# A planned order with a quiet time for attention products during each slot scatter, other planner constants, and second blocks of 288 rows

## The chip, the cores and the metric

One core of one Trainium2 chip runs the whole program in one launch. The metric is the device time of that launch in microseconds (us); the median of the runs counts. The engines are called PE (matrix products), PEld (the loading of PE's stationary operand), DVE (vector), ACT (scalar), POOL (GpSimd) and SP (the engine that issues most DMAs).

## The reference

Three computations follow each other. Shapes: attention on 4 batches, 8 heads, 768 positions of 48 numbers; 3072 tokens of 384 numbers after it; all float32.

```python
for t in range(S):                                   # delta-rule attention, k_n = k / norm
    y[:, :, t] = einsum('bhd,bhde->bhe', q[:, :, t], state)
    v_old = einsum('bhde,bhd->bhe', state, k_n[:, :, t])
    state = state + beta_t * einsum('bhd,bhe->bhde', k_n[:, :, t], v[:, :, t] - v_old)

h = x @ w_in                                         # first MoE: 384 -> 2048 -> 384
x = where(h > 0, h, exp(min(h, 0)) - 1) @ w_out

noisy = x @ w_gate + log1p(exp(x @ w_noise)) * noise # second MoE: 8 experts, top 2
top2, top2_w = two largest of noisy, softmax of the two
for e in range(8):                                   # 384 -> 1024 -> 384 for the rows sent to e
    out[rows of e] += top2_w * (maximum(x[rows of e] @ w1[e], 0) @ w2[e])
```

## The kernel before, in words

The tokens are cut into six groups of 512 (g = 0 to 5), 128 positions of the sequence each. A group passes through these stages.

**Attention.** `front(g)` prepares a group: gram products of the keys (`grams`, matmul at L467), a triangular solve on DVE (`solve`, L514 and L517, 30 steps, and the transposes at L522 and L524), and two merges of the halves of the solution on PE (L548 and L564). `chain(g, c)` then goes through two chunks c of 64 positions: products with the state (S, L634; U, L652), the update of the state (L668) and the outputs (Y, L693), with DVE and ACT work in between (L639, L641, L657, L675). These are many very small matmuls: a gram is 128 of them, a U or a state update 64.

**First MoE.** For each of 16 slices f of the hidden width a step makes nine matmuls (`l1`, L712) into one bank, an activation on ACT and DVE (`elu`, L717 to L735), and the products with w_out (`l2`, L760, L764 and L765, three for each 128 rows). Groups 0 and 1 are worked in halves of 256 rows for f below 8. w_out is split once into two parts, stored to `wod` in DRAM (L390) and read back as `wo` tiles (L383) by `feed`, all of it on the SP queue.

**Routing.** `routing(g)` transposes the rows (L802), makes the gate scores, picks the two best experts on DVE, makes a running count (L876) and, from it, the slot of each row by two matmuls (L880, L881). GpSimd then writes the slots with eight indirect DMAs (L912). The order of the groups is 1, 0, 2, 3, 4, 5.

**Second MoE.** Each expert has room for 832 rows, in blocks of 512 and 320 (`BLK`); a loop for more rows (`overflow`) stands behind and does not run with these inputs, whose counts per expert are 743 to 797. For a block SP fetches the slots as `ids` (L990, L991, L993), GpSimd gathers the rows of x2d into `xg` by up to four indirect DMAs (L998), PE transposes them (L1012), ACT and DVE split them (L1015, L1017), and eight steps of L1 (L712), relu (L745, L750) and L2 follow; in a last chunk of fewer than 128 rows the high and low parts stand side by side in one stationary operand (L760, L762). `combine` scales the rows and adds them to the output through GpSimd (L1041). The first block needs the slots of groups 0 to 4 only, the second blocks those of all six.

**What sets the order.** Nothing is scheduled on the chip. While the program is built, the class `Sched` keeps a clock for PE, ACT and DVE from assumed costs, and takes at each point, among the jobs that could go on, the one that could start first (within `NEAR`) and has the lowest rank. Products have a kind: 0 dense, 1 attention, 2 transposes and routing. The order in which PE, ACT, DVE, POOL and SP get their instructions is the order in which the planner sent the jobs on, and each engine executes its own list in that order. The constants at the head (`FRONT`, `CONV`, `ROUTE`, `EVAC`, `EW`, `RP`, `TURN`, `DMA_RATE`, `EARLY`) are ranks and assumed costs: a new value means another order, not other work.

Of the kernel before, what the change touches and what calls it, by code (L numbers as in the profile page):

```python
# [12 lines left out]
AF = mybir.ActivationFunctionType  # L13
# [4 lines left out]
B, H, S, D = 4, 8, 768, 48  # L18
DM, F1, E, F2 = 384, 2048, 8, 1024
NT = B * S  # L20
NG = 6
# [4 lines left out]
HALF = NP // 2  # L26
NOUT = NT + NPAD
ES = 3200
BLK = (512, 320)
CAP = sum(BLK)  # L30
FRONT = (1, 1.02, 2.68, 3, 3, 3)
ATT = (1, 1, 1, 1, 1, 1)
CONV = (2, 2.5)
NEAR = 0.1
ROUTE = 2.44
EVAC = 1.39
EW = 5.99
AHEAD = 4
DMA_RATE = 0.226
LAG = 2  # L40
EARLY = {6: 8, 8: 9, 10: 10, 12: 11, 21: 12, 23: 13, 25: 14, 27: 15}
RP = 0.61
TURN = 0.25
FETCH = 3.7

F64_TINY = 2.0 ** -15 * 1.125
# [1 line left out]
def PE(cost, *after, n=0, kind=1, m=5, rank=99):  # L48
    return "PE", cost, after, n, kind, rank, (2, 4, 2)[kind] * m
# [7 lines left out]
def wait(*after):  # L57
    return None, 0.0, after, 0, 0, 99, 0
# [30 lines left out]
class Sched:  # L89
# [7 lines left out]
    def __init__(self):  # L97
        self.clock = {"PE": 0.0, "ACT": 0.0, "DVE": 0.0}
        self.words, self.lines = 0, {0: 0.0, 1: 0.0}
        self.jobs, self.count, self.kind, self.banks, self.got, self.now, self.wire = [], 0, 0, [0.0, 0.0], None, 0.0, 0.0  # L100

    def add(self, job, rank):
        self.count += 1
# [10 lines left out]
    def start(self, step):  # L114
        engine, cost, after, n, kind, _, words = step
        t = self.clock[engine] if engine else 0.0
        for a in after:
            if a is not None and not isinstance(a, float):
                a = a.t
            if a is None:  # L120
                return None
            t = max(t, a)
        if n:
            free = sorted(b for b in self.banks if b is not None)
            if len(free) < n:
                return None
            t = max(t, free[n - 1])
        if words:
            t = max(t, self.lines[(self.words + words) // 256] - 0.5)
        return t  # L130
# [59 lines left out]
class Kernel:  # L190
# [81 lines left out]
    def init_out(self):  # L272

        S, m = self.S, 3 * NOUT // 128
        out = self.out.rearrange("(p m) d -> p (m d)", m=NOUT // 128).rearrange("p (m d) -> p m d", d=128)
        yield wait(self.attended[2])
        for i in range(0, m, 15):
            yield wait(S.now + 12.0)
            S.dma(0.98)
            self.nc.sync.dma_start(out[:, i:i + 15], self.zero[:, None, :].to_broadcast([128, 15, 128]))  # L280


    def moe1_alloc(self):
# [75 lines left out]
    def feed(self):  # L359

        nc, S = self.nc, self.S
        x, v = [t.rearrange("p a b -> p (a b)") for t in self.xtile(1, I32)], self.V.rearrange("p c a b -> p (c a b)")
        places = [t[:, 2 * DM * i:2 * DM * i + 2 * DM].bitcast(I32) for t in (*x, v) for i in range(2)]
        places = [places[(f % 4) if f < 12 else 4 + f % 2] for f in range(NP)]
        stored, dead, order = [Event() for _ in range(NP)], [Event() for _ in range(NP)], []
        for n, (*_, f) in enumerate(self.steps):
            order.append((f, n))
            if n in EARLY:
                order.append((EARLY[n], None))
        done = set()  # L370
        for f, n in order:
            if f in done:
                yield wait(self.rw.need(), stored[f])
            else:
                yield wait(self.rw.need(), *([dead[f - 4]] if 4 <= f < 12 else [self.attended[1], *([dead[f - 2]] if f > 13 else [])]
                                             if f >= 12 else []))
            wo, ready, used = self.work.tile([128, 2, DM], FR, name="wo", bufs=4), Event(), self.rw.take()
            if n is not None:
                self.wos[n] = wo, ready, used
                self.fed[n].t = S.now  # L380
            flat = wo.rearrange("p a d -> p (a d)").bitcast(FT)
            if f in done:
                nc.sync.dma_start(flat, self.wod[f])  # L383
                ready.t = S.dma(0.4)
                continue
            done.add(f)
            nc.sync.dma_start(places[f], self.w_out[128 * f:128 * f + 128].bitcast(I32))

            def end(t, f=f, n=n, ready=ready, used=used, flat=flat):
                nc.sync.dma_start(self.wod[f], flat)  # L390
                ready.t, stored[f].t = t, S.dma(0.4)
                if n is None:
                    used.t = stored[f].t
                if f == 11:
                    self.xfree.t = t
                if f == NP - 1:
                    self.load_v(2)
            S.add(self.convert(places[f], wo[:, 0], wo[:, 1], DM, S.dma(0.4), dead[f], end), CONV[f >= 8])

# [354 lines left out]
    def l2(self, gh, gl, wh, wl, acc, n, first, last):  # L754

        nc = self.nc
        nw = wh.shape[-1]
        for t, a in enumerate(acc):
            o = slice(128 * t, 128 * t + 128)
            nc.tensor.matmul(a[:, :nw], gh[:, o], wh, start=first, stop=False)  # L760
            if o.stop > n:
                nc.tensor.matmul(a[:, :nw], gh[:, o], wl, start=False, stop=last)  # L762
            else:
                nc.tensor.matmul(a[:, :nw], gh[:, o], wl, start=False, stop=False)  # L764
                nc.tensor.matmul(a[:, :nw], gl[:, o], wh, start=False, stop=last)  # L765

# [10 lines left out]
    def x2_out(self, g, acc, held, e):  # L777
        nc = self.nc
        for t, (a, free) in enumerate(zip(acc, held)):
            f = yield DVE(0.56, e, self.rx.need()) if g == 0 else ACT(0.49, e, self.rx.need())  # L780
            x2, used = self.x2s()
# [6 lines left out]
            self.x2[g].append((x2, used, f))  # L788
            r0 = NPAD + 512 * g + 128 * t
            nc.sync.dma_start(self.x2d[r0:r0 + 128, :], x2)  # L790
        self.S.add(self.routing(g), 0.5 if g == NG - 1 else ROUTE)

    def gates(self, g):
        nc, S = self.nc, self.S
# [35 lines left out]
    def routing(self, g):  # L830
# [43 lines left out]
        for b in range(1, B):  # L874
            V.tensor_add(ex[:, b], ex[:, b - 1], m[:, b - 1])
        V.tensor_add(self.cum, ex[:, B - 1], m[:, B - 1])  # L876
        e = yield PE(0.1, e, n=1, kind=2)
        k = self.S.got[0]
        pp = self.bank(k)[:, :B * E]
# [54 lines left out]
        if g == NG - 2:  # L934
            self.adj = self.consts.tile([128, E], FT, name="adj")
            V.tensor_scalar(self.adj, pc, -1.0, float(BLK[0]), op0=OP.mult, op1=OP.add)
            V.tensor_scalar(self.adj, self.adj, 0.0, None, op0=OP.max)
        self.routed[g].t = e + 20.0
        self.listed[g].t = e


# [62 lines left out]
    def gathered_t(self, n, xg, xh, xl, at=None):  # L1004
        nc, S = self.nc, self.S
        for t, x in enumerate(xg):
            e = yield PE(0.35, *([at + 1.0 * t] if at else []), n=1, kind=2)
            k = S.got[0]
            m = min(128, n - 128 * t)
            pt = self.bank(k)[:, :DM].rearrange("p (k m) -> p k m", k=3)  # L1010
# [10 lines left out]
    def gather(self, e, i, xs, out):  # L1021
        yield wait(self.routed[NG - 1 if i else NG - 2])
        out.ids, xg = self.fetch(e, i)
        out.t = yield from self.gathered_t(BLK[i], xg, *xs, self.S.now + 8.0)

    def combine(self, n, ids, acc, held=None, e=0.0):
        nc = self.nc
        puts = []
        for t, a in enumerate(acc):
# [1 line left out]
            f = yield DVE(0.6, e)  # L1031
            y = self.m2.tile([128, DM], FT, name="y", bufs=4)
            if m < 128:
                nc.scalar.activation(y[:m], a[m:, :DM], AF.Copy)
                nc.vector.tensor_add(y[:m], y[:m], a[:m, :DM])
                a = y
            nc.vector.tensor_scalar(y[:m], a[:m, :DM], ids.bitcast(FT)[:m, t, 1:2], None, op0=OP.mult)  # L1037
# [225 lines left out]
```

## Time and profile before

| what | value |
|---|---|
| runs | 1235.65, 1234.97, 1241.44 us; median 1235.65 us |
| the profiled execution | 1239.07 us, its span 1237.3 us |
| mean granted TensorE clock | 0.950 of full speed |
| busy in the span | PE 1076.2, PEld 963.6, DVE 717.5, ACT 491.4, POOL 210.4 us |

The span runs from the first to the last instruction of the profiled execution; 1.8 us of its own time lie outside. All terms are taken from that execution. Busy time of PE is given by modelled ends, so a stretch with PE busy in all of its 25 us has no gap that the profile sees.

### The profile page before, as it was taken

How to read it: one execution, taken by the hardware profiler on the slowest of the kernel's cores; microseconds unless marked ns; L12 is line 12 of the kernel's file. 1: busy time of each engine (PE TensorE's matmuls, PEld its weight loads, DVE VectorE, ACT ScalarE, POOL GpSimd, SP SyncE). 2: the span in 40 equal slices, each digit the busy share in tenths (PEclk: the TensorE clock that was granted, in tenths of full speed). 3: DMA queues.
4: the chain of work that ended last, by engine and by line, in shares of the span. 5: the costliest groups of instructions: out<-in, count | busy, mean ns of one | idle time of the engine just before them, and what ended most of it. 6: DMA issues, size and time to landing. Idle time of an engine off the chain costs nothing.

```text
span 1237.3 us, 28286 instructions
## 1 busy us (share of the span) xinstructions
PE 1076.2 (87%) x11780; PEld 963.6 (78%) x11780; DVE 717.5 (58%) x1832; ACT 491.4 (40%) x979; POOL 210.4 (17%) x282
## 2 busy tenths in 40 slices
PE   1173859679997999979989998999999999999995
PEld 1163759568885888868878887889898989899995
DVE  9979898796354894867453644534535353434321
ACT  2343744735633338425625544123424232323210
POOL 3000000000002020020020041424242323232412
PEclk9997789689998999989998998999999999999998
DMA  9123444642367354225223453135654452524313
GB/s 270 32 79 91 168 162 122 226 172 78 101 184 192 87 146 123 66 63 157 65 66 127 147 138 113 14 90 90 169 113 98 89 139 47 145 42 100 48 16 39
DMA packets 93241, 136.55 MB, mean 110 GB/s; under 512 B 35056, under 2 KB 63472, under 8 KB 92528
## 3 DMA queue, kind: packets, MB, share of 16 engines
q1 hardware_dynamic: 80560, 114.14, 31.8%
q0 software_dynamic: 12544, 20.51, 9.8%
q8 instruction: 95, 1.56, 0.5%
q14 instruction: 42, 0.34, 0.1%
HBM read 108.02 MB, written 26.60 MB: 109 GB/s over the span
## 4 chain that ended last, share of the span: by engine, by line
PE 76%; DVE 13%; ACT 3%; issue 3%; DMA 2%; another core or an unknown queue 1%; POOL 0%; SPq 0%; POOLq 0%; DVEq 0%; ACTq 0%
PE ht L712 31%; PE acc L760 12%; PE acc L765 10%; PE acc L764 10%; PE att L693 3%; DVE TR L514 2%; DVE L L517 2%; PE att L634 2%; PE att L652 2%; PE att L467 2%; PE att L1012 1%; DMA xg<-x2d,ids 1%; PE acc L762 1%; DMA V<-in_w_out_dram 1%
## 5 line engine op out<-in xcount | busy, mean ns | idle before, releaser
L712 PE MATMUL ht<-xh,w 128*128 128x512 f32 (+2 forms) x1056 | 326.7, 369 | 6.1 <-ACT w L314 4.0
L712 PEld LDWEIGHTS ht<-xh,w 128*128 128x128 f32 x1056 | 195.0, 192 | 37.8 <-issue 5.2
L750 DVE SCALAR_TENSOR_TENSOR gl<-ht,gh 128x512 fp32r<-128x512 f32 (+1 forms) x128 | 71.4, 558 | 246.9 <-ACT gh L745 239.5
L712 PE MATMUL ht<-xl,w 128*128 128x512 f32 (+2 forms) x528 | 191.6, 363 | 2.2 <-issue 2.2
L745 ACT ACTIVATE gh<-ht 128x512 fp32r<-128x512 f32 (+1 forms) x128 | 66.4, 519 | 281.6 <-PE ht L712 243.9
L760 PE MATMUL acc<-wo,gh 128*128 128x384 f32 x384 | 140.6, 366 | 10.6 <-DMA wo<-wod 9.7
L765 PE MATMUL acc<-wo,gl 128*128 128x384 f32 x384 | 133.6, 348 | 0.0
L764 PE MATMUL acc<-wo,gh 128*128 128x384 f32 x384 | 133.0, 346 | 0.0
L727 DVE SCALAR_TENSOR_TENSOR e<-e,ht 128x512 f32<-128x512 f32 (+1 forms) x112 | 67.8, 608 | 109.0 <-ACT e L725 106.0
L1041 POOL DMA_INDIRECT out_dram<-y,ids x56 | 88.8, 1586 | 218.5 <-DVE y L1037 208.3
L723 ACT ACTIVATE e<-ht 128x512 f32<-128x512 f32 (+1 forms) x112 | 59.8, 536 | 150.7 <-PE ht L712 140.2
L712 PE MATMUL ht<-xh,ew 128*128 128x320 f32 (+1 forms) x384 | 115.7, 359 | 1.0 <-ACT xh L1015 1.0
L712 PEld LDWEIGHTS ht<-xl,w 128*128 128x128 f32 x528 | 101.5, 192 | 12.5 <-issue 2.3
L912 POOL DMA_INDIRECT slots<-pr,si x48 | 47.8, 996 | 358.3 <-DVE si L907 282.2
L733 ACT ACTIVATE gh<-e 128x512 fp32r<-128x512 f32 (+1 forms) x112 | 63.4, 570 | 79.5 <-DVE e L727 78.1
L760 PEld LDWEIGHTS acc<-wo,gh 128*128 128x128 f32 x384 | 75.2, 196 | 17.3 <-issue 7.4
L735 DVE TENSOR_TENSOR gl<-e,gh 128x512 fp32r<-128x512 f32 (+1 forms) x112 | 68.3, 613 | 30.7 <-ACT gh L733 25.8
L760 PE MATMUL acc<-w,gh 128*128 128x384 f32 x224 | 76.8, 343 | 0.9 <-issue 0.9
L712 PEld LDWEIGHTS ht<-xh,ew 128*128 128x128 f32 x384 | 70.2, 190 | 9.0 <-ACT xh L1015 1.5
L760 PE MATMUL acc<-ew,gh 128*128 128x384 f32 x224 | 77.1, 344 | 0.0
L764 PEld LDWEIGHTS acc<-wo,gh 128*128 128x128 f32 x384 | 75.6, 197 | 1.3
L765 PEld LDWEIGHTS acc<-wo,gl 128*128 128x128 f32 x384 | 75.3, 196 | 0.0
(190 smaller groups left out, 2045.7 us busy)
## 6 DMA issues: line engine op xcount, KB each, us to landing
wo<-wod SPq DMA_DIRECT2D x104, 384.0 KB
ws<-in_w_dram SPq DMA_DIRECT2D x48, 256.0 KB
ws<-in_w_dram SPq DMA_DIRECT2D x64, 192.0 KB
wod<-wo SPq DMA_DIRECT2D x16, 384.0 KB
out_dram<-zero SPq DMA_DIRECT2D x5, 960.0 KB
Kt<-in_kt_dram SPq DMA_DIRECT2D x12, 384.0 KB
w<-in_w_in_dram SPq DMA_DIRECT2D x9, 512.0 KB
SQ<-in_qt_dram SPq DMA_DIRECT2D x24, 192.0 KB
```

The costliest lines, as they stand in the source:

```text
L712: nc.tensor.matmul(ph[:, :n], w(kk, f), x[:, kk, o:o + n], start=(i == 0), stop=(i == 8))
L723: nc.scalar.activation(x, ph[:, :n], AF.Exp)
L727: nc.vector.scalar_tensor_tensor(x, x, -1.0, ph[:, :n], op0=OP.mult, op1=OP.max)
L733: nc.scalar.activation(gh, x, AF.Copy)
L735: nc.vector.tensor_sub(gl, x, gh.bitcast(FT))
L745: nc.scalar.activation(gh[:, :n], ph[:, :n], AF.Relu)
L750: nc.vector.scalar_tensor_tensor(d, ph[:, o], 0.0, gh[:, o].bitcast(FT), op0=OP.max, op1=OP.subtract)
L760: nc.tensor.matmul(a[:, :nw], gh[:, o], wh, start=first, stop=False)
L764: nc.tensor.matmul(a[:, :nw], gh[:, o], wl, start=False, stop=False)
L765: nc.tensor.matmul(a[:, :nw], gl[:, o], wh, start=False, stop=last)
L912: x = nc.gpsimd.indirect_dma_start(out=self.slots[:, :], out_offset=bass.IndirectOffsetOnAxis(ap=si[:, t, b:b + 1], axis=0), in_=pr[:, b, ...
L1041: x = nc.gpsimd.indirect_dma_start(out=self.out[:, :], out_offset=bass.IndirectOffsetOnAxis(ap=ids[:m, t, 0:1], axis=0), in_=y[:m], in_off ...
```

## The change

There are four parts.

1. **A quiet time.** When a routing has updated its running count, the planner notes its time plus `QUIET` = 14 us, and plans no product of kind 1 (attention) before that.
2. **The routing of group 4** gets the rank 0.5 that only group 5 had; the time at which its slots count as readable is `e + 13.0` instead of `e + 20.0`, the transposes of gathered rows are planned from 7 us after the fetch, 1.3 us apart, instead of 8 us and 1.0 us.
3. **Second blocks of 288 rows** instead of 320, with the last chunk's stationary operand cut to the 64 columns that hold data (2 x 32).
4. **Other constants** of the planner, the store of w_out's split parts as a job of its own (`store`, planned 0.21 us before the parts are ready, and so behind DMAs that were sent before it), and the zeros of the output written in 15 pieces, 9 us apart, instead of 5 pieces, 12 us apart.

```diff
-BLK = (512, 320)
+BLK = (512, 288)
-FRONT = (1, 1.02, 2.68, 3, 3, 3)
+FRONT = (1, 1.02, 2.68, 3, 0.62, 3)
-CONV = (2, 2.5)
+CONV = (1.82, 2.5)
-ROUTE = 2.44
-EVAC = 1.39
-EW = 5.99
+ROUTE = 3.7
+EVAC = -0.4
+EW = 4.15
-DMA_RATE = 0.226
+STORE = -0.21
+QUIET = 14.0
+DMA_RATE = 0.244
-EARLY = {6: 8, 8: 9, 10: 10, 12: 11, 21: 12, 23: 13, 25: 14, 27: 15}
-RP = 0.61
-TURN = 0.25
+EARLY = {6: 8, 8: 9, 10: 10, 12: 11, 21: 12, 23: 13, 26: 14, 29: 15}
+RP = 0.91
+TURN = 0.6
...
+        if kind == 1:
+            t = max(t, self.quiet)
...
-        for i in range(0, m, 15):
-            yield wait(S.now + 12.0)
-            S.dma(0.98)
-            self.nc.sync.dma_start(out[:, i:i + 15], self.zero[:, None, :].to_broadcast([128, 15, 128]))
+        for i in range(0, m, 5):
+            yield wait(S.now + 9.0)
+            S.dma(0.33)
+            self.nc.sync.dma_start(out[:, i:i + 5], self.zero[:, None, :].to_broadcast([128, 5, 128]))
...
-            def end(t, f=f, n=n, ready=ready, used=used, flat=flat):
+            def store(t, f, n, used, flat):
+                yield wait(t + STORE)
                 nc.sync.dma_start(self.wod[f], flat)
-                ready.t, stored[f].t = t, S.dma(0.4)
+                stored[f].t = S.dma(0.4)
                 if n is None:
                     used.t = stored[f].t
+
+            def end(t, f=f, n=n, ready=ready, used=used, flat=flat):
+                ready.t = t
+                S.add(store(t, f, n, used, flat), 1)
...
-            nc.tensor.matmul(a[:, :nw], gh[:, o], wh, start=first, stop=False)
             if o.stop > n:
-                nc.tensor.matmul(a[:, :nw], gh[:, o], wl, start=False, stop=last)
+                m = 2 * (n - o.start)
+                o = slice(o.start, o.start + m)
+                nc.tensor.matmul(a[:m, :nw], gh[:, o], wh, start=first, stop=False)
+                nc.tensor.matmul(a[:m, :nw], gh[:, o], wl, start=False, stop=last)
             else:
+                nc.tensor.matmul(a[:, :nw], gh[:, o], wh, start=first, stop=False)
...
-        self.S.add(self.routing(g), 0.5 if g == NG - 1 else ROUTE)
+        self.S.add(self.routing(g), 0.5 if g >= NG - 2 else ROUTE)
...
         V.tensor_add(self.cum, ex[:, B - 1], m[:, B - 1])
+        self.S.quiet = self.S.now + QUIET
...
-        self.routed[g].t = e + 20.0
+        self.routed[g].t = e + 13.0
...
-            e = yield PE(0.35, *([at + 1.0 * t] if at else []), n=1, kind=2)
+            e = yield PE(0.35, *([at + 1.3 * t] if at else []), n=1, kind=2)
...
-        out.t = yield from self.gathered_t(BLK[i], xg, *xs, self.S.now + 8.0)
+        out.t = yield from self.gathered_t(BLK[i], xg, *xs, self.S.now + 7.0)
...
-                nc.scalar.activation(y[:m], a[m:, :DM], AF.Copy)
+                nc.scalar.activation(y[:m], a[m:2 * m, :DM], AF.Copy)
```

**PE after the slot products of group 1's routing.** `att` tiles are the two banks of attention and routing; `ht` is a bank of L1, `acc` of L2. Before (L467 are grams, L668 the update of the state):

```order
L881 MATMUL att_4849<-rex,ones 128x32
L712 MATMUL ht<-xh_2165,w_124 128x512
...
L760 MATMUL acc<-wo,gh 128x384
...
L467 MATMUL att_4914<-Kt_105 32x64 x2
...
L668 MATMUL att_4994<-Ub,Ktm 48x48 x2
```

After the change (L894 is the old L881, L721 the old L712, L775 the old L760, L814 the old L802, L677 the old L668):

```order
L894 MATMUL att_4713<-rex,ones 128x32
L721 MATMUL ht<-xh_2149,w_123 128x512
...
L775 MATMUL acc<-wo,gh 128x384
...
L814 MATMUL att_4781<-ident,x2s 128x128 x3
L721 MATMUL ht<-xh_2149,w_124 128x512
...
L814 MATMUL att_4800<-ident,x2s 128x128 x3
...
L814 MATMUL att_4826<-ident,x2s 128x128 x3
...
L677 MATMUL att_4842<-Ub,Ktm 48x48 x2
```

Before, one L1 and one L2 stood between the slot products and the grams. Now three L1, two L2 and three transposes stand ahead of the first attention product, a state update, and the grams come later still. After the slot products of group 2, too, dense steps now stand where the S products stood, and the first attention product behind them is a merge, as it is after those of group 0. The attention products that stood behind the slot products of group 3 (U, L652, and Y, L693) now stand ahead of them; only dense steps follow there.

**SP around the first two fetches of slots**, at the passage from the first to the second MoE; `ws` are raw pieces of expert weights. Before:

```order
L383 DMA wo<-wod 128x768 x10
L993 DMA ids<-slots 128x4x2
L965 DMA ws<-in_w_dram 128x512 x3
L965 DMA ws<-in_w_dram 128x384 x4
L965 DMA ws<-in_w_dram 128x512 x2
L993 DMA ids<-slots 128x4x2
```

After the change (L387 is the old L383, L978 the old L965, L1006 the old L993):

```order
L387 DMA wo<-wod 128x768 x8
L1006 DMA ids<-slots 128x4x2
L387 DMA wo<-wod 128x768 x3
L978 DMA ws<-in_w_dram 128x512 x3
L978 DMA ws<-in_w_dram 128x384
L1006 DMA ids<-slots 128x4x2
```

The first fetch now stands three `wo` loads, that is three dense steps, ahead of the end of the first MoE; the second behind three `wo` and four `ws` loads instead of nine `ws`. On PE the four transposes of the first block, which before stood in a row ahead of its L1, now stand between half steps of the last group.

**PE at the merges of group 2's front**, still among the half steps of group 1 (L548 and L564 are the merges, L467 the grams of group 3). Before:

```order
L712 MATMUL ht<-xh_2165,w_123 128x256
L548 MATMUL att_2724<-TR,TB_108 32x32 x2
...
L564 MATMUL att_2801<-GD,TR 32x32 x2
...
L467 MATMUL att_2897<-Kt_111 32x64 x2
...
L760 MATMUL acc<-wo,gh 128x384
```

After the change (L557 and L573 are the merges, L476 the grams):

```order
L721 MATMUL ht<-xh_2149,w_123 128x256
L557 MATMUL att_2817<-TR,TB_108 32x32 x2
...
L775 MATMUL acc<-wo,gh 128x384
...
L573 MATMUL att_2946<-GD,TR 32x32 x2
...
L775 MATMUL acc<-wo,gh 128x384
...
L476 MATMUL att_3079<-Kt_111 32x64 x2
```

Before, the first merge, the second and the grams followed each other. Now two half steps, each an L1 and an L2, stand between the merges, and two more between the second merge and the grams.

## Rows read from the trace of the kernel before

**Rows 1.** The page: busy time of each engine, and shares of the chain that ended last.

```profile
PE 1076.2 (87%) x11780; PEld 963.6 (78%) x11780; DVE 717.5 (58%) x1832; ACT 491.4 (40%) x979; POOL 210.4 (17%) x282
...
PE 76%; DVE 13%; ACT 3%; issue 3%; DMA 2%; another core or an unknown queue 1%; POOL 0%; SPq 0%; POOLq 0%; DVEq 0%; ACTq 0%
```

**Rows 2.** Stretches of 25 us: stretch, then busy us of each engine, granted clock, DMA.

```profile
225.00:250.00 25.00, 17.50 (x395) 16.44 (x386) 21.70 (x56) 17.61 (x37) 0.00 (x0) 0.69 0.56 201
...
275.00:300.00 25.00, 25.00 (x245) 22.26 (x239) 21.32 (x46) 9.10 (x16) 0.00 (x0) 0.87 0.22 65
...
450.00:475.00 25.00, 25.00 (x247) 22.16 (x246) 18.18 (x38) 14.67 (x24) 9.22 (x16) 1.00 0.86 198
...
725.00:750.00 25.00, 21.03 (x94) 17.02 (x92) 11.95 (x21) 13.16 (x25) 6.38 (x7) 0.86 0.70 206
750.00:775.00 25.00, 23.52 (x141) 21.12 (x142) 8.72 (x15) 10.52 (x24) 1.98 (x3) 0.93 0.19 63
```

**Rows 3.** Timeline of POOL, slot writes of groups 1 and 2: start, length, [idle before].

```profile
387.01 1.15 POOL L912 DMA_INDIRECT slots<-pr,si  x1 [29.24 <-DVE si L907]
...
396.31 0.97 POOL L912 DMA_INDIRECT slots<-pr,si  x1 [0.22 <-issue]
...
538.54 0.96 POOL L912 DMA_INDIRECT slots<-pr,si  x1 [0.22 <-issue]
```

**Rows 4.** Timeline of PE after group 1's slot products, until the outputs begin.

```profile
384.27 0.19 PE L880 MATMUL att<-rm,tri 128*128 128x32 bf16 x1
...
388.70 0.66 PE L467 MATMUL att<-Kt 48*32 48x64 f32 x44
389.76 0.25 PE L467 MATMUL att<-Kt 48*32 48x32 f32 x3 [0.40 <-issue]
...
407.37 0.41 PE L693 MATMUL att<-AQ,Ub 128*64 128x64 f32 x4
```

**Rows 5.** Timeline of PE: attention products that fall in no scatter.

```profile
340.40 0.94 PE L668 MATMUL att<-Ub,Ktm 64*48 64x48 f32 x64
...
376.38 2.07 PE L652 MATMUL att<-V,TB 64*64 64x48 f32 x64
...
380.69 1.43 PE L467 MATMUL att<-Kt 48*32 48x64 f32 x128
```

**Rows 6.** Timeline of PE after group 2's slot products.

```profile
531.70 1.18 PE L634 MATMUL att<-SQ,Kt 48*64 48x128 f32 x32
...
542.08 2.53 PE L634 MATMUL att<-SQ,Kt 48*64 48x128 f32 x32 [4.88 <-DVE AQ L641]
...
548.08 0.40 PE L712 MATMUL ht<-xh,w 128*128 128x512 f32 x1
```

**Rows 7.** Timeline of PE after group 3's slot products.

```profile
641.81 1.59 PE L652 MATMUL att<-V,TB 64*64 64x48 f32 x47
...
658.39 0.34 PE L693 MATMUL att<-AQ,Ub 128*64 128x64 f32 x4
```

**Rows 8.** Timeline of the SP queue before the second MoE begins.

```profile
718.29 12.94 SPq L383 DMA_DIRECT2D wo<-wod  x4
731.29 1.18 SPq L993 DMA_DIRECT2D ids<-slots  x1
732.52 11.15 SPq L965 DMA_DIRECT2D ws<-in_w_dram  x9
```

**Rows 9.** Chain that ended last, expert L1: two blocks' steps, start and length.

```profile
1126.06 2.10 PE ht L712 x9
1130.28 2.10 PE ht L712 x9
...
1142.73 1.33 PE ht L712 x9
```

**Rows 10.** Timeline of PE at group 2's merges and group 3's grams.

```profile
221.38 0.31 PE L564 MATMUL att<-GD,TR 32*32 32x32 f32 x4 [3.43 <-ACT TR L554]
...
230.02 0.42 PE L467 MATMUL att<-Kt 48*32 48x64 f32 x4 [4.08 <-ACT TB L575]
```

**Rows 11.** Timeline of PE at the first merge of group 5's front.

```profile
579.41 0.24 PE L548 MATMUL att<-TR,TB 32*32 32x32 f32 x2 [2.12 <-issue]
```

More of the change, by code (lines that the diff above doesn't have):

```diff
@@ L99, in __init__ @@
         self.words, self.lines = 0, {0: 0.0, 1: 0.0}
-        self.jobs, self.count, self.kind, self.banks, self.got, self.now, self.wire = [], 0, 0, [0.0, 0.0], None, 0.0, 0.0
+        self.jobs, self.count, self.kind, self.banks, self.got, self.now, self.wire, self.quiet = [], 0, 0, [0.0, 0.0], None, 0.0, 0.0, 0.0
     def add(self, job, rank):
```

## Prediction, made before the changed kernel ran

> **What bounds the kernel now.** I read the page first. PE is busy for 1076.2 us of the 1237.3 us span, and 76% of the chain that ended last lies on PE [rows 1]; the question is where the other 161 us lie. The table of 25 us stretches answers it [rows 2]. Up to about 275 us PE is not full while DVE has little to spare (in 225 to 250, PE 17.50, DVE 21.70, clock 0.69): the solves of the fronts set the pace. From 275 on most stretches have PE at 25.00. There a gain comes only from less PE work, or from the few stretches in which PE stands still or runs below full clock.
>
> Those are four: three after routings, one at the passage to the second MoE. I went to them with the timelines. GpSimd writes the slots of group 1 in eight transfers from 387.01 to 397.28, some 1.3 us apart, and those of group 2 until 539.50 [rows 3]. In that time PE passes 44 gram products at speed (0.66 us), and then only a few at a time, "issue" before them: it waits for no semaphore, but for its next instructions [rows 4]. Dense steps alone do not suffer: in 450 to 475 GpSimd is busy for 9.22 us with the slots of group 0, and PE has 25.00 at clock 1.00 [rows 2]. So what starves is the stream of very small products, which needs many instructions per microsecond.
>
> **The three scatter stalls.** Undisturbed, 128 grams take 1.43 us, a state update 0.94, a U 2.07 [rows 5].
> Group 1: from the first gram (388.70) to the outputs (407.37) 18.7 us pass [rows 4]. The work there is grams 1.43, update 0.94 and an L1; an L1 takes 2.10, and as a dense step takes 4.22, an L2 2.12 [rows 9]. Sum 4.5; lost 14.2.
> Group 2: 531.70 to 548.08, 16.4 us, for two S groups (1.18 each, the first one's time), L1 and L2: 6.6; lost 9.8 [rows 6]. Most is one gap of 4.88 behind DVE, itself late, and a second S group that took 2.53.
> Group 3: 641.81 to 658.39, 16.6 us, for U 2.07, L1, L2 and a group of outputs, taken like an S group at 1.18: 7.5; lost 9.1 [rows 7].
> Together 33.1 us. The new order puts dense steps there, or ends the attention earlier. No PE work is added: the dense steps come sooner, the products later.
>
> **What of it stays.** After group 1's slot products three L1, two L2 and three transposes precede the first attention product: 10.5 us and about 1 (three transposes at the planner's assumed 0.35) make 11.6. The last write ended 397.28 - 384.27 = 13.0 us after them [rows 3, 4]. So the first products still meet the last write or two, there, after group 2 and, newly, after group 0, where a merge now stands some 11 us behind. From below this costs nothing, since 44 products passed at speed. From above it costs the rest of the writes, up to 3 us a place, about 10 in all. I take 4, nearer the short gaps of [rows 4] (0.40 each).
>
> **The passage to the second MoE.** In 725 to 775 PE lacks 3.97 + 1.48 = 5.5 us, and the clock is short of full by (0.14 + 0.07) x 25 = 5.3 us, partly while PE idled anyway [rows 2]: about 10 us in all. The first fetch of slots waits behind four loads of `wo`, 12.94 us of the queue, and the second behind nine of `ws`, 11.15 us [rows 8]. Loads of `wo` go one to a dense step, so three fewer ahead bring the first gather some 12.7 us sooner, well over the wait. The second fetch passes five `ws`, half of its queue time. I take 8 of the 10; the ends are 4 (the first stretch's gap alone) and 10.7. The new rank of group 4's routing serves the same gap: it only makes the slots ready for the earlier fetch, so it has no term of its own.
>
> **288 columns.** An L1 of 512 columns takes 2.10, of 320 1.33 [rows 9]; the slope is 0.0040 us per column, so 32 fewer save 0.128 in each of 8 x 8 = 64 L1: 8.2 us. In proportion it would be 0.133, 8.5. I take 8.3, with 6 as lower end should weight loads begin to show. L2 keeps its count and its 384 moving columns: nothing. Room for 800 rows holds the largest count, 797, so the loop for more rows does not run.
>
> **The early stage.** Around group 2's merges PE waited 3.43 us for ACT, and 4.08 before the grams [rows 10]. Two half steps (2.1 us each at the L1 and L2 prices) now stand at each of these places, and the clock, 0.69 in that stretch [rows 2], should fall less. But DVE stays nearly full until 300, and dense steps use it too. What can be gained is solve work that moves behind 275, where PE is the bound. I take 8. The ends are 15 (all of the 7.5 us gap of 225 to 250, and as much by the clock) and a loss of 3, as w_out's stores and the small zero fills now stand elsewhere on SP among the `wo` loads.
>
> **The late fronts.** Front 5's first merge already waits 2.12 us [rows 11]. Its attention products are pushed back by each quiet time, and I count 3 us for a longer wait there (0 to 6). Other new constants only reorder jobs that lie under PE work; I give them nothing.
>
> **Sum.** 1239.07 - 33.1 + 4 - 8 - 8.3 - 8 + 3 = 1188.7 us for the profiled execution. That execution lies 3.4 above the median 1235.65; for the median I predict **1185 us**. All good ends together give 67 less, all bad ends 24 less: 1168 to 1212 for the median.
>
> **The rivals.**
> *A, the stalls only move.* The planner's clock is not the chip's. If routing or the writes run 2 or 3 us later than planned, each of three places meets several writes, stands for them, and follows at a low clock, as after group 1. The part of a stall that comes after the writes was (407.37 - 397.28) - 4.5 = 5.6 us in group 1 at the least [rows 3, 4]; with 2 to 3 us of writes that is 8 a place, 24 instead of my 4: 1205. For it: the margin of 13.0 to 11.6 is on the wrong side. Against: the late products are few. Chance 0.20.
> *B, slower than before.* Each quiet time pushes the chain of attention back by some 11 us. If front 5 and its chain then end after group 4's dense steps, PE has nothing left to put between. The place is group 5's first merge [rows 11]. Three pushes would be 35 us of waits, and as much again at half the speed behind them: 1185 + 70 = 1255. It decides from the point at which the waits, with the clock, pass 51 us. Against it: from 300 on the stretches have much free DVE time on the whole, and the order leaves dense steps between front 5's merges. Chance 0.05.
> *C, the products are not short of instructions*, and something else in those stretches delays them; then moving them gains nothing: 33.1 - 4 = 29 less gain, 1214. For it speaks that a gap in group 2 ends on DVE [rows 6]; against it the short runs with "issue" before them [rows 4], and the full stretch with dense work [rows 2]. Chance 0.08.
> The Trainium skill (Runtime: NRT & Kernel Launch, section on instruction fetch mechanics) says that a sequencer fetches its next page by its own DMA queue while it executes, mostly hidden, because dispatch is slower than the fills. By that rule C would hold. The short runs of [rows 4] disagree for products this small, so the sum goes by the rows.
>
> **Chances.** My forecast has 0.67, A 0.20, C 0.08, B 0.05. The range of 1168 to 1216 takes in the forecast's ends, A and C, and leaves out B and what of the early stage could be worse. About 0.5%, 6 us, is what a measurement of this kernel can tell from no change. A and C are faster by far more; a tenth of the bad ends could meet in no change. Faster 0.91, same 0.04, slower 0.05.
>
> **What would show it.** In the new profile, the stretches that hold the writes of groups 1, 2 and 3 should have PE near 25.00 and clock 1.00, with any "issue" gaps only at the last writes; A would show bursts there, and a low clock behind. The first gather should wait 12 us less, and PE lack under 2 us at the passage. L1 of the second blocks should take 1.20. In 200 to 275 PE should lack some 8 us less. The forecast is wrong if small products behind the writes still come in bursts of more than 3 us, if PE idles at front 5's merges by over 6, or if the early stage ends no sooner.

## The result, and the profile after the change

The changed kernel takes 1200.95 us in the median of four runs (1198.58 to 1201.85); the kernel before took 1235.31 beside it. The ratio is 0.9712, with a 95% interval of 0.9673 to 0.9752: 34 us faster. The forecast was 1185, its range 1168 to 1216. The sign and the large terms were near; one term, what stays of the stalls, was four times too small.

The profiled execution took 1201.85 us, its span is 1200.0: 37.3 less than before. Its page, busy time of each engine:

```profile
PE 1060.9 (88%) x11780; PEld 948.4 (79%) x11780; DVE 713.4 (59%) x1832; ACT 488.5 (41%) x979; POOL 211.0 (18%) x282
```

PE is busy for 15.3 us less than before [rows 1], and its idle time fell from 161 to 139 us. The stretches of 25 us (busy us of PE, PEld, DVE, ACT and POOL, then the granted clock) show where it still stands:

```profile
225.00:250.00 25.00, 19.32 (x343) 18.96 (x344) 15.72 (x32) 16.12 (x32) 0.00 (x0) 0.77 0.61 217
...
375.00:400.00 25.00, 23.42 (x342) 20.10 (x341) 9.07 (x16) 9.97 (x21) 8.29 (x16) 0.93 0.44 89
450.00:475.00 25.00, 24.48 (x265) 21.41 (x267) 18.50 (x58) 16.17 (x30) 6.25 (x11) 1.00 0.58 149
475.00:500.00 25.00, 22.11 (x411) 18.42 (x409) 8.95 (x17) 12.52 (x23) 3.31 (x6) 0.86 0.29 57
...
575.00:600.00 25.00, 22.64 (x348) 19.63 (x351) 8.19 (x15) 11.25 (x20) 1.52 (x4) 0.86 0.20 62
700.00:725.00 25.00, 23.45 (x122) 20.58 (x120) 10.29 (x17) 11.99 (x21) 6.32 (x7) 1.00 0.63 162
725.00:750.00 25.00, 24.94 (x155) 21.97 (x155) 13.84 (x30) 14.68 (x32) 1.89 (x3) 1.00 0.40 127
```

Beside [rows 2]: 225 to 250 has gained a little in PE and clock; the passage, now in 700 to 750, lacks 1.6 us in place of 5.5 and keeps its clock at 1.00. But 475 to 500 and 575 to 600 are new in this list: PE 22.11 and 22.64 at clock 0.86. They hold the ends of the slot writes of groups 0 and 2. POOL's first and last write for group 0:

```profile
467.65 1.29 POOL L925 DMA_INDIRECT slots<-pr,si  x1 [82.84 <-DVE si L920]
...
477.29 1.36 POOL L925 DMA_INDIRECT slots<-pr,si  x1 [0.21 <-issue]
```

PE's timeline at that place (start, length, operation, count, idle before). L573 is the second merge:

```profile
474.84 0.50 PE L573 MATMUL att<-GD,TR 32*32 32x32 f32 x35
476.29 0.18 PE L573 MATMUL att<-GD,TR 32*32 32x32 f32 x1 [0.96 <-issue]
...
479.21 1.34 PE L573 MATMUL att<-GD,TR 32*32 32x32 f32 x80 [0.47 <-issue]
480.48 0.80 PE L721 MATMUL ht<-xh,w 128*128 128x512 f32 x1
...
484.49 0.52 PE L775 MATMUL acc<-wo,gh 128*128 128x384 f32 x1
...
487.04 0.49 PE L814 MATMUL att<-ident,x2s 128*128 128x128 f32 x3
```

35 products of the merge pass at speed, 13 more come in four short runs while the last writes go out, and the 80 at the end follow the last write. The L1 behind them takes 4.01 us (480.48 to 484.49) in place of 2.10. From 474.84 to the transposes at 487.04 12.2 us pass for a merge of about 1.4, an L1 and an L2 (2.10 and 2.12 [rows 9]): 6.6 lost. Group 0 lost nothing before. The same after groups 1 (from the state update, L677, to the grams) and 2 (from the merge to the transposes):

```profile
383.19 0.90 PE L677 MATMUL att<-Ub,Ktm 64*48 64x48 f32 x29
...
390.36 1.43 PE L476 MATMUL att<-Kt 48*32 48x64 f32 x128
...
574.38 0.40 PE L573 MATMUL att<-GD,TR 32*32 32x32 f32 x25
...
576.45 0.28 PE L573 MATMUL att<-GD,TR 32*32 32x32 f32 x4 [1.17 <-issue]
577.89 1.54 PE L573 MATMUL att<-GD,TR 32*32 32x32 f32 x95 [1.17 <-issue]
...
585.98 0.49 PE L814 MATMUL att<-ident,x2s 128*128 128x128 f32 x3
```

Group 1: 7.2 us for a state update of 0.94 [rows 5] and an L2: 4.1 lost. Group 2: 11.6 us for a merge, L1 and L2: 6.0 lost. So 16.7 us stay, where 33.1 were lost before [rows 4, 6, 7]: 10.2 while the attention products themselves run, and 6.5 in the dense steps behind them, at a lower clock.

The passage: the first fetch of slots on SP and the first gathered transposes on PE:

```profile
702.60 0.38 SPq L1006 DMA_DIRECT2D ids<-slots  x1
...
711.10 0.52 PE L1025 MATMUL att<-ident,xg 128*128 128x128 f32 x3 [1.54 <-DMA xg<-x2d,ids]
```

The fetch starts 28.7 us earlier than the 731.29 of [rows 8], in a program that is 22.6 us ahead at the first expert product; the wait for the rows is 1.54 us. An L1 of 288 columns on PE, with the L2 behind it:

```profile
1119.77 0.30 PE L721 MATMUL ht<-xh,ew 128*128 128x288 f32 x1
...
1120.96 0.34 PE L775 MATMUL acc<-ew,gh 128*128 128x384 f32 x1
```

It takes 1.19 us to the first product of the L2; forecast was 1.20.

In the early stage, PE's wait at the second merge [rows 10] is gone and its waits for ACT before the grams have halved (2.5 us in 100 to 300, in place of 4.9), but its waits for `wo` have doubled. Before, and after (us in total, times, longest):

```profile
PE acc L760 <- DMA wo<-wod: 9.7, 2, 5.0
```

```profile
PE acc L775 <- DMA wo<-wod: 21.5, 3, 9.8
```

The longest, on SP's and PE's timelines:

```profile
154.88 14.19 SPq L395 DMA_DIRECT2D wod<-wo  x3
169.20 0.86 SPq L387 DMA_DIRECT2D wo<-wod  x2
...
172.90 0.66 PE L775 MATMUL acc<-wo,gh 128*128 128x384 f32 x1 [9.77 <-DMA wo<-wod]
```

SP stands for 14 us in three stores of split w_out that wait for DVE, and the load that PE needs stands behind them.

### The profile page after: what moved, and what is told of

It reads as the page before. It is cut to its first block, busy times and chain, and to the rows that moved or that the text cites. A ratio compares the mean times of both kernels' runs of the same rounds, so it can differ in the third digit from the quotient of the medians.

```text
span 1200.0 us, 28295 instructions
## 1 busy us (share of the span) xinstructions
PE 1060.9 (88%) x11780; PEld 948.4 (79%) x11780; DVE 713.4 (59%) x1832; ACT 488.5 (41%) x979; POOL 211.0 (18%) x282
## 4 chain that ended last, share of the span: by engine, by line
PE 77%; DVE 12%; ACT 3%; DMA 3%; issue 3%; POOL 0%; SPq 0%; POOLq 0%; DVEq 0%; ACTq 0%
PE ht L721 32%; PE acc L775 11%; PE acc L777 10%; PE acc L776 10%; PE att L702 2%; DVE TR L523 2%; DVE L L526 2%; PE att L643 2%; PE att L661 2%; PE att L1025 2%; PE att L476 1%; PE acc L772 1%; PE acc L773 1%; PE att L573 1%; DMA xg<-x2d,ids 1%
## 5 line engine op out<-in xcount | busy, mean ns | idle before, releaser
L721 PE MATMUL ht<-xh,w 128*128 128x512 f32 (+2 forms) x1056 | 327.3, 370 | 3.5 <-ACT w L318 3.5
L721 PEld LDWEIGHTS ht<-xh,w 128*128 128x128 f32 x1056 | 197.0, 195 | 35.0 <-ACT w L318 3.8
L721 PE MATMUL ht<-xl,w 128*128 128x512 f32 (+2 forms) x528 | 191.8, 363 | 0.7 <-issue 0.7
L775 PE MATMUL acc<-wo,gh 128*128 128x384 f32 x384 | 141.3, 368 | 21.5 <-DMA wo<-wod 21.5
L721 PEld LDWEIGHTS ht<-xl,w 128*128 128x128 f32 x528 | 103.1, 195 | 11.1 <-issue 0.9
L721 PE MATMUL ht<-xh,ew 128*128 128x288 f32 (+1 forms) x384 | 110.0, 348 | 0.0
L775 PEld LDWEIGHTS acc<-wo,gh 128*128 128x128 f32 x384 | 76.1, 198 | 29.0 <-issue 18.6
L721 PEld LDWEIGHTS ht<-xh,ew 128*128 128x128 f32 x384 | 68.6, 188 | 8.5
L1011 POOL DMA_INDIRECT xg<-x2d,ids x56 | 55.3, 987 | 93.4 <-DMA ids<-slots 60.4
L775 PE MATMUL acc<-w,gh 128*128 128x384 f32 x192 | 66.2, 345 | 0.5 <-issue 0.5
```

Of the source, the lines that this page charges most:

```text
L721: nc.tensor.matmul(ph[:, :n], w(kk, f), x[:, kk, o:o + n], start=(i == 0), stop=(i == 8))
L1011: nc.gpsimd.indirect_dma_start(out=x[:m], out_offset=None, in_=self.x2d[0:rows, :], in_offset=bass.IndirectOffsetOnAxis(ap=ids[:m, t, 0:1] ...
```

## The experiments

The runs went to several chips. On most of them the kernel before takes 1232 to 1244 us; these are called the 1235 chips below, and the trace of the changed kernel above is from one of them. On the chip of runs 1 to 4 (q0b apart) it takes 1210.27, in one run; this is the 1210 chip. So each run is compared with runs of its own set, or up to the same place of the program: the start of the first expert product (L1 of the first block) is the mark. On the 1235 chips the changed kernel reaches it at 722.93 and 721.78, the kernel before at 745.53 and 747.31.

**1. The writes of group 0 held back (late0).** They stand behind those of group 2 in POOL's queue, and the tiles that hold them get a third buffer (not shown in the cut).

```diff
...
+        if g == 0:
+            self.kept = [(si, pr)]
+        for si, pr in [] if g == 0 else [*self.kept, (si, pr)] if g == 3 else [(si, pr)]:
             for b in range(B):
                 for t in range(2):
...
```

> The changed kernel, with the eight slot writes of group 0 held back and issued with those of group 3, where only dense steps run; the order on PE is the same. Theory (the writes starve PE of instructions): the 6.6 us that were lost from 474.84 to 487.04 go, and the 16 writes in a row after group 3's slot products leave dense steps at 25.00 of 25; time about 1195 (1193 to 1198). Rival 1 (the merge is slow there for a reason of its own: DVE, ACT or its banks): the gap stays and the time with it, 1200 to 1202. Rival 2 (dense steps run out of instructions too, only later): the gain is given back after group 3.

It took 1189.27 on the 1210 chip. It reached the mark at 708.82; the run with 320 rows on the same chip (4, below), whose order up to there is the changed kernel's, at 709.15. So holding the writes gained nothing there, and the reason is that nothing was lost: the run with 320 rows, with group 0's writes in 466.77 to 477.8, has PE at

```profile
450.00:475.00 25.00, 24.46 (x330) 21.28 (x331) 18.03 (x59) 16.92 (x30) 6.91 (x13) 1.00 0.59 148
475.00:500.00 25.00, 25.00 (x504) 21.51 (x505) 14.79 (x32) 15.53 (x30) 2.65 (x4) 1.00 0.31 71
```

against 24.48 and 22.11, the latter at a clock of 0.86, on the 1235 chip. Between the theory and rival 1 the run therefore does not decide. For the 1210 chip it answers rival 2. Its writes of group 2 and then of group 0, and PE meanwhile:

```profile
557.74 0.96 POOL L928 DMA_INDIRECT slots<-pr,si  x1 [174.81 <-DVE si L920]
...
572.76 0.96 POOL L928 DMA_INDIRECT slots<-pr,si  x1 [4.66 <-DMA slots<-pr,si]
...
565.76 1.80 PE L573 MATMUL att<-GD,TR 32*32 32x32 f32 x128
```

```profile
550.00:575.00 25.00, 24.93 (x274) 21.78 (x276) 12.86 (x44) 18.17 (x34) 10.84 (x20) 1.00 0.51 112
575.00:600.00 25.00, 25.00 (x411) 20.68 (x402) 10.62 (x24) 9.79 (x18) 6.63 (x13) 1.00 0.30 66
```

Under 16 writes in 25 us dense steps stay full, and on this chip even 128 merge products among them take 1.80 us. On the 1235 chip only the eight writes of group 3 fall in a stretch of dense steps after the change: PE has 25.00 and 24.90 in 625 to 675.

**2. No quiet time (q0, and q0b on a 1235 chip).**

```diff
-QUIET = 14.0
+QUIET = 0.0
```

> The changed kernel with a quiet time of 0 instead of 14. Theory: small products stand among the writes of groups 1, 0 and 2 again and lose about what they lost before the change, 33 us in place of the 16.7 that three shorter stalls still cost: 1214 to 1220. Rival (the other constants, not the quiet time, moved the products): below 1206.

> The changed kernel with a quiet time of 0, again, on this job's chip. On the chip of the first job it reached the first expert product 9.3 us later than the changed order did (718.4 against 709.15 with 320 rows). Theory (the quiet time saves what the stalls cost, and that differs from chip to chip): 14 to 18 us later than the changed kernel where the kernel before takes 1235 to 1240, so 1214 to 1220. Rival (the quiet time is worth the same everywhere): 1208 to 1212.

On the 1210 chip, for which the first forecast was not made: 1197.18, the mark at 718.40, 9.3 us later than with the quiet time. On a 1235 chip: 1217.84, the mark at 736.22, 14.4 us later than the changed kernel's 721.78 on another such chip, and 16.6 later than the 719.61 of run 8 on the same chip, whose order on PE is the changed kernel's. The stretch of group 1's writes on the one chip and on the other:

```profile
375.00:400.00 25.00, 21.83 (x482) 18.38 (x479) 13.12 (x43) 10.97 (x24) 9.28 (x16) 0.93 0.39 83
```

```profile
375.00:400.00 25.00, 18.66 (x344) 15.05 (x339) 5.98 (x21) 6.92 (x16) 8.79 (x16) 0.80 0.24 60
```

and one of ten short runs of grams in the second:

```profile
387.18 0.43 PE L476 MATMUL att<-Kt 48*32 48x64 f32 x4 [1.11 <-issue]
```

The quiet time does what it was said to do, and is worth 9 us on the one chip and 14 to 17 on the other. The rival of a fixed worth falls, and with 1217.84 so does the first one (below 1206).

**3. A longer quiet time (q21).**

```diff
-QUIET = 14.0
+QUIET = 21.0
```

> The changed kernel with a quiet time of 21 instead of 14: by the order the first attention product stands 17.7 us of dense work or more behind the slot products of groups 1, 0 and 2, where the last write ended up to 15.7 us after them. Theory: all three remaining stalls go, 16.7 us: 1184 to 1190. Rival (attention is now so late that a wait on DVE or ACT takes the place of the stalls): 1195 or more, with idle time of PE before merges or state products.

1203.45 on the 1210 chip, the mark at 724.84, 15.7 us later than with 14 (709.15, run 4). The rival holds: from 300 to the mark PE waits for ACT 12.0 us in all, in run 4 not at all. 8.1 us of it stand ahead of attention and routing products and come from ACT's work on attention and L1, much as the rival said. The other 3.9 come from a wait that I had not named: the order now puts the transposes of a routing right behind the rows' store to DRAM, and ACT must not overwrite the rows before it has landed. ACT during group 0's writes, and the two largest of PE's waits for ACT (us in total, times, longest):

```profile
473.88 0.49 ACT L816 ACTIVATE x2s<-att 128x384 f32<-128x384 f32 x1 [6.03 <-DMA x2d<-x2s]
```

```profile
PE att L814 <- ACT x2s L816: 3.2, 3, 1.7
PE att L893 <- ACT TB L584: 2.7, 1, 2.7
```

On this chip the three stalls are small; what 21 does on a 1235 chip is not shown.

**4. Second blocks of 320 rows (blk320).**

```diff
-BLK = (512, 288)
+BLK = (512, 320)
```

> The changed kernel with second blocks of 320 rows. By the slope of L1 (0.128 us for 32 columns, 64 times) it is 8.2 us longer, 1209 to 1211. Rival (weight loads or L2 hide the shorter products): 0 to 3 us longer.

1195.13; from the mark to the end of the span 484.2 us, against 478.7, 477.0 and 476.8 in the three other runs of the set: 5.5 to 7.4 us for the 32 columns, 8.2 by the slope. The forecast holds, a little too high.

**5. Both kernels again (after2, before2).** Unchanged.

> The changed kernel again, as the reference for the other runs of this job, since a job's chip can differ from the first one's. Theory (the stalls after the routings differ from chip to chip, nothing else does): the time up to the first expert product is near 709, as with 320 rows on the chip of the first job, if the kernel before takes about 1210 here, and near 723 if it takes about 1235. Rival (another part differs, such as the early stage): the stretches before 300 differ too.

> The kernel before again, with a profile on this job's chip. Theory: where it takes about 1210, its stalls after the routings of groups 1, 2 and 3 (14.2, 9.8 and 9.1 us on the first chip) are shorter by 20 to 25 us together, and the passage and the early stage are as before. Rival: the early stage or the passage gives the difference.

1202.32 and 1241.54, the mark at 721.78 and 747.31: the set had a 1235 chip. So there is no profile of the kernel before on the 1210 chip. For the changed order there is one in run 4: up to 300 its stretches are those of the 1235 chip within 1 us of PE, and after the routings they differ.

**6. Stores as before (storeback).**

```diff
-                S.add(store(t, f, n, used, flat), 1)
+                nc.sync.dma_start(self.wod[f], flat)
+                stored[f].t = S.dma(0.4)
+                if n is None:
+                    used.t = stored[f].t
```

> The changed kernel with each store of split w_out issued as soon as it was before, not as a job of its own. Theory (three waits of PE for wo, 21.5 us in place of 9.7, come from stores that stand on SP ahead of loads and wait for DVE): PE's waits for wo fall below 12 us and the kernel is 5 to 12 us faster than the changed one on this chip. Rival (DVE sets the early pace, and a wait taken away comes back as another): within 2 us of it.

1222.31, 20 us slower than the changed kernel on this chip, and the waits for `wo` did not fall:

```profile
PE acc L778 <- DMA wo<-wod: 22.2, 4, 10.0
```

The theory that the new job made these waits falls. The planner's order moved with the edit, so the 20 us are not those of the stores alone. Some 6 us lie before 300, where PE is busy for 182.6 us in place of 188.7. Most of the rest lies after the routings: by the order the first attention products stand 8.5 to 10.9 us behind the slot products in place of 11.1 to 11.4, the writes begin 5.4 to 5.6 us behind them in place of 3.1 to 4.2, and the products stall for longer, as in these rows of grams after group 0 (the third of five short runs of 2 to 4, and the 70 that follow):

```profile
481.85 0.43 PE L479 MATMUL att<-Kt 48*32 48x32 f32 x4 [1.19 <-issue]
...
486.14 1.18 PE L479 MATMUL att<-Kt 48*32 48x32 f32 x70 [1.10 <-issue]
```

**7. Group 4's routing as before (rank).**

```diff
-        self.S.add(self.routing(g), 0.5 if g >= NG - 2 else ROUTE)
+        self.S.add(self.routing(g), 0.5 if g == NG - 1 else ROUTE)
-        self.routed[g].t = e + 13.0
+        self.routed[g].t = e + 20.0
```

> The changed kernel with the old rank of group 4's routing and the old time at which its slots count as readable, so that the first fetch of slots stands two wo loads later on SP, behind ten. Theory (the fetch's place sets the wait at the passage): PE waits again for the first gathered rows, 3 to 8 us longer than the changed kernel on this chip. Rival (a margin was there): within 1.5 us of it.

1207.76, 5.4 slower than the changed kernel in the same set. The fetch starts at 707.95, and PE waits for the rows, then for their evacuation:

```profile
707.95 0.43 SPq L1006 DMA_DIRECT2D ids<-slots  x1
...
717.82 0.52 PE L1025 MATMUL att<-ident,xg 128*128 128x128 f32 x3 [1.86 <-DMA xg<-x2d,ids]
...
724.70 0.49 PE L721 MATMUL ht<-xh,ew 128*128 128x512 f32 x1 [1.19 <-ACT xh L1028]
```

The theory holds, within its 3 to 8 us, with one run of each: 2.9 us of the 5.4 lie before the mark (724.70 against 721.78) and the rest behind it, while from 300 to 700 PE idles for 9.6 us here and 9.7 there. The earlier routing is what lets the fetch go early.

**8. All writes after the attention (held).** As in 1, for groups 1, 0 and 2, in POOL's list behind group 3's routing.

```diff
...
+        self.kept = [*getattr(self, "kept", []), (si, pr)]
+        for si, pr in self.kept if g > 2 else []:
             for b in range(B):
                 for t in range(2):
...
+        if g > 2:
+            self.kept = []
```

> The changed kernel with the slot writes of groups 1, 0 and 2 held back and issued in a row, 32 of them, with those of group 3, where only dense steps follow; the order on PE is the changed kernel's. Theory (only products of attention next to the writes suffer): after the routings of groups 1, 0 and 2 PE has 25.00 of 25 and clock 1.00, the 32 writes leave dense steps full, and the 16.7 us that three stalls cost on the first chip go: about 1185 on a chip on which the kernel before takes 1235 to 1240, and 2 to 6 us off on one on which it takes 1210. Rival 1 (dense steps run dry in 41 us of writes): up to 10 us are given back between 640 and 685. Rival 2 (the products are late for a reason of their own): no gain.

1200.08: no test of the theory, for the edit held nothing. POOL's first write of group 1, and of group 0:

```profile
372.38 1.16 POOL L927 DMA_INDIRECT slots<-pr,si  x1 [22.24 <-DVE si L920]
...
464.48 1.29 POOL L927 DMA_INDIRECT slots<-pr,si  x1 [81.94 <-DVE si L920]
```

The writes are later in POOL's list, but nothing stands ahead of them in it, so they start as soon as their slots are there. In run 1 group 2's writes stood ahead, and those wait. What writes would do that are really held till the attention is over is not shown.

**9. Stores on GpSimd's queue (storepool), and with 8 (both).**

```diff
-                nc.sync.dma_start(self.wod[f], flat)
+                nc.gpsimd.dma_start(self.wod[f], flat)
```

> The changed kernel with the 16 stores of split w_out issued by GpSimd's queue, idle then, so that SP never stands in a store that waits for DVE. The order on PE is the changed kernel's. Theory (the 20.5 to 21.5 us in which PE waits for wo before 300 come from these stores): the waits fall below 6 us, the stretch up to 300 ends 6 to 13 us sooner, and the time falls by as much. Rival (DVE sets the early pace, so that the parts themselves come late): the waits stay above 15 us, or come back as waits for DVE and ACT, and the time stays within 3 us.

> Both edits: slot writes held back to group 3's, and the stores of w_out on GpSimd's queue. Theory: the gains add, 1185 less 6 to 13, 1172 to 1179 where the kernel before takes 1235 to 1240. Rival: one of the two is given back, 1185 or more.

1197.52, the mark at 717.13. PE's waits in 100 to 300:

```profile
PE ht L721 <- DVE e L736: 8.6, 2, 5.9
PE acc L775 <- DMA wo<-wod: 5.9, 1, 5.9
```

The waits for `wo` fall from 20.1 us in run 8, on the same chip, to 5.9, but the mark comes only 2.5 us sooner than the 719.61 of that run (4.7 sooner than in run 5, on another chip): 8.6 us come back as waits for DVE. The theory holds for the waits, the rival for the time. With edit 8, which held nothing, it is the same kernel in time, and took 1200.19 in four runs (1198.54 to 1201.78), ratio 0.9697 (0.9668 to 0.9726) against the changed kernel's 0.9712 (0.9673 to 0.9752): a gain is not shown.

## Why the prediction was right, and where it was wrong

The terms against the profiled execution, in us (the first counts the old stalls as gone whole, so that what stands there now is all in the second):

| term | forecast | measured |
|---|---|---|
| stalls after groups 1, 2 and 3, old form | -33.1 | -33.1 |
| what stays of them | +4 | +16.7 |
| passage | -8 | about -8 |
| 288 columns | -8.3 | -7 |
| early stage and late fronts | -5 | -5.9 (what is left of the sum) |
| sum | -50.4 | -37.3 |

**What bounds the kernel, and the scatter stalls.** Right: from 275 on PE is full outside the places named, and taking the quiet time out puts the stalls back (2). That dense steps do not suffer holds for stretches of dense steps, not for an L1 right behind small products (last section). Rival C, that moving the products gains nothing, falls by the same runs. Whether the products are short of instructions is another matter (below).

**What of it stays: the step that failed.** The place was right, three routings, group 0 newly among them; the size was not. I counted 1.4 us of writes that the products would still meet, and priced only these. Two things were missed. The writes began later behind the slot products than the 2.7 us that group 1 had shown [rows 3, 4]: after group 0, 4.1 us behind them (PE's last at 463.50), with the last at 478.65 in place of 476.5. And each stall dragged the clock down after it: the L1 or L2 behind it ran for some 4 us at half speed (window 475 to 500, clock 0.86), though rival A had this very price, 8 a place. What came is A at 5.6 a place: the 10.2 us of stalls alone are already the upper end that I had named, "about 10", and the clock's 6.5 come on top. By the prediction's own sign, bursts of more than 3 us, this part failed: the short runs fill 3.9 us after group 0 (475.34 to 479.21) and 3.1 after group 2 (574.78 to 577.89). Run 6 shows how steep this is: with 0.5 to 3 us less of dense work ahead, and writes that begin up to 2.5 us later, PE idles 8.0 us longer in 300 to 700 and loses 5.0 us more by the clock than in run 5, 13 of its 20 us.

**The passage.** Right: of the 10 us of gap and clock [rows 2] 1.6 is left, at full clock. Taking one part back (7) returns 5.4 of the 8. The mark agrees: from it to the end the changed kernel takes 477.1 us in place of 491.8, 14.7 less, of which 7.3 to 9.2 are left for the passage when the columns have their 5.5 to 7.4.

**288 columns.** Right; 7 in place of 8.3, from the upper end of run 4. An L1 that takes 1.19 in place of 1.33 would give 9 in 64 of them, so the term is known to some 2 us.

**Early stage and late fronts.** The sum is near by two errors. Front 5's wait [rows 11] did not grow by 3, it went: no PE gap above 0.3 us is left in 500 to 575. The rest, about 4 in place of 8, is all that the early stage gave. It is what the other terms leave of the 37.3, and the stretches agree: up to 300 PE is busy for 187.2 us in place of 183.2, and in 200 to 275 it lacks 4.2 us less, not 8. The wait at the merge went as forecast, of that before the grams half, but SP's stores came in ahead of loads of `wo`, and where these waits are taken away (9) waits for DVE take most of it. "DVE stays nearly full until 300" was the right bound, and I should have let it weigh more.

**Rival B** did not come with 14. With 21 (3) late attention did cost time, 15.7 us up to the mark and not 70, by waits for ACT (12.0 us), none of them at group 5's first merge, the place that I had named; and that kernel is still faster than the one before (1203.45 against 1210.27).

## What to carry to other kernels

A planner's pause is as long as its assumed costs make it: read in the next trace where the transfers end and where the held work begins, and price what overlaps with the clock's loss behind it, not by its own length. Moving work back in a queue's order delays it only if something ahead of it waits (8). When a wait on one queue is taken away in a stretch that an engine bounds, expect a part of it: here 2.5 us of 14.2 (9).

## What the runs showed of the hardware that was not expected

**Chips differ here by some 2%.** The kernel before takes 1210.27 on one chip, in one run, and 1232 to 1244 on the others. In the changed order the difference up to the mark, 709.15 against 721.78, lies in the stretches with slot writes, where small products pass on the one chip and stall on the others, at the same pace of the writes (one in 1.27 us). The cause of that is open. The change is worth some 21 us on that chip by run 1 (1210.27 to 1189.27), and 34 to 39 on the others.

**In the stall of group 0 the products are not held by the fetch of their page.** I had written that they wait for their next instructions. In the changed kernel's trace the DMA queues between 465.50 and 481.00, with the stall and the whole merge in it, are these:

```profile
q1 hardware_dynamic: 1903, 2.04, 73.0%
q0 software_dynamic: 242, 0.01, 1.1%
```

There is no packet of the two instruction queues among them, which have 95 and 42 packets in the program; yet all 128 products of the merge ran in that time, so their page had come earlier. This agrees with the Trainium skill (Runtime: NRT & Kernel Launch, section on instruction fetch mechanics), which calls the fetch mostly hidden; only the inference I drew from it for rival C, that moving the products gains nothing, does not hold.

**More than the start of small products is held.** In the kernel before, under the writes of group 2, the dense L1 right behind an S group came in pieces too, with four gaps of 0.32 to 0.47 us. Its first and last line, and what DVE and ACT did then ("remote": the profile finds no releaser on this core):

```profile
533.20 0.40 PE L712 MATMUL ht<-xh,w 128*128 128x512 f32 x1 [0.32 <-issue]
...
536.81 0.39 PE L712 MATMUL ht<-xh,w 128*128 128x512 f32 x1 [0.47 <-issue]
...
541.24 0.35 DVE L639 TENSOR_TENSOR V<-V,att 128x192 f32<-128x192 f32 x1 [7.79 <-remote]
...
541.40 0.60 ACT L723 ACTIVATE e<-ht 128x512 f32<-128x512 f32 x1 [10.06 <-remote]
```

By the program DVE waits here for the S group, whose last product ends at 532.88, and ACT for the L1, which ends at 537.20 (both ends modelled). Both go on only 1.7 to 1.9 us after the last write (539.50 [rows 3]). Under the writes of group 0, with dense steps alone, ACT takes up an L1 0.04 us after its modelled end twice (452.70, 456.91) and 1.0 us after it once. So the gap of 4.88 us "behind DVE" [rows 6] seems to be one of PE's own results that came late, which a lack of instructions on PE does not explain. That PE's results are held with its products is read from the profile and not tested.

What holds them is open. Full DMA engines alone do not: the 128 grams of 380.69 [rows 5] pass at speed with a DMA share of 1.00 (window 380.69 to 382.10). And not every such gap has a write beside it: that of [rows 11], 2.12 us, and one of 2.10 us in run 4, before 388.85, have none. The Trainium skill (NOTIFIC — the notification-queue block, section on overflow) says that the path for an engine's records can stall the engine that makes them; no run here shows whether that happens.
